# Sliding-window attention and a squared-ReLU feed-forward on one core: engine order from a list schedule, two batches turned on TensorE, two tiles in 128-token units, loads two batches ahead

## The chip, the cores and the metric

The kernel runs on one core of a Trainium2 chip. The core has TensorE (PE: matmuls, with its weight loads shown apart as PEld), VectorE (DVE), ScalarE (ACT), GpSimd (POOL) and SyncE (SP). Each engine takes its instructions strictly in program order, and semaphores order the engines against each other. Here POOL issues the loads from device memory, which turn float32 into bfloat16 on the way, and SP issues the copies inside the core's memory and the stores. The metric is device time in microseconds (us), lower is better. The kernel before takes 404.95 us, the median of 3 runs (404.74 to 405.19).

## The reference

Eight batches of 576 tokens with 8 heads of 64 go through attention in which a token sees the 32 tokens on either side of it. Its output, 4608 tokens by 512, goes through a feed-forward layer of width 2048.

```python
def _attn_ref(q, k, v):
    B, H, S, D = q.shape            # 8, 8, 576, 64
    scores = np.matmul(q, k.transpose(0, 1, 3, 2)) / np.sqrt(D)
    mask = np.abs(pos[:, None] - pos[None, :]) <= 32
    ...
    return np.matmul(attn, v)       # attn: softmax over the masked scores

def _moe_ref(x, w_in, w_out):       # x: 4608 x 512, w_in: 512 x 2048, w_out: 2048 x 512
    h = x @ w_in
    r = np.maximum(h, 0.0)
    return (r * r) @ w_out
```

## The kernel before

**Attention** goes in 72 steps, nine per batch, each for 64 query tokens and all heads. For a step, `scores(n)` makes four PE matmuls into one of two PSUM banks (`sc`), ACT takes the exponential, DVE multiplies by a mask into `pt`. `av(n)` makes eight matmuls with the values into the single bank `avp`; the last column of the values is one, so that the sums of the softmax come with it. DVE then takes reciprocals (`rs`) and scales (`xr`). `xturn(n)` turns the result by two PE transposes into `trp`, and ACT copies it to `xt`, which holds the tokens along the free axis.

**Queries and keys** must lie with the head's dimension on the partitions. A batch is loaded as rows by eight DMAs of POOL (`load_qk`, tiles `qraw`, `kraw`, two buffers), turned in 32x32 blocks by eight DVE stream transposes (`turn`, into `qst` and `kst`), and spread to its place by twelve DMAs of SP (`spread`, into `qz` and `kt`). The first `sc` matmul of a batch needs all twelve. Values need no turn: four DMAs to `vd` and two to `vx`, and SP copies the rest of `vx` out of `vd` (`copy_v`), since even steps need the rows shifted by 64.

**Feed-forward** goes in nine tiles of 512 tokens. `mm1(T, d)` makes four matmuls of 512 columns for one of 16 blocks of the width, ACT applies the ReLU (`rt`), DVE squares it (`gt`). `mm2(T, u, seg)` makes a quarter of the 16 matmuls that give 128 output tokens; after the last quarter ACT copies the bank (`oe`) and SP stores it. A unit of either is four matmuls.

**The order** is the order in which `build` records the operations; `rec` derives the waits from the tiles that are read and written, and `emit` writes the instructions out. In step n, `build` records `scores(n)`, one stream transpose of the next batch, a feed-forward unit, `xturn(n-2)`, a unit, `av(n-1)`, and two units. A unit of tile T may be recorded only once all eight steps of its tokens are through (`moe_items`), and `mm2` of a tile stands beside `mm1` of the next. At the start come the fills, the loads of batch 0, the fills of masks and identity, both weight matrices, and then the whole of batch 0's turns and spreads. Batch b+1 is loaded, as recorded, at steps 0 and 1 of batch b.

Of the kernel before, what the change touches and what calls it, by code (L numbers as in the profile page):

```python
# [3 lines left out]
ALU = mybir.AluOpType  # L4
# [12 lines left out]
VS = D_ + 2  # L17
KW = 32 + S_ + 32
LAST_MM = 16


class Op:
    __slots__ = ("eng", "fn", "deps", "same", "inc", "val", "sem", "dma")


class Prog:
# [3 lines left out]

    def __init__(self, nc):
        self.nc = nc
        self.ops = []
        self.writer = {}
        self.readers = {}
        self.dsem = {}

    def rec(self, eng, fn, reads=(), writes=(), dma=None):
        op = Op()
        op.eng, op.fn, op.dma = eng, fn, dma  # L40
        op.deps, op.same = set(), set()
        op.inc, op.val, op.sem = False, None, None
        for r in reads:
            for w in self.writer.get(r, ()):
                op.deps.add(w)
        for t in writes:
            for w in self.writer.get(t, ()):
                if not (w.eng == eng and w.dma is None and dma is None):
                    op.deps.add(w)
            for r in self.readers.get(t, ()):  # L50
                if not (r.eng == eng and r.dma is None):
                    op.deps.add(r)
        op.deps.discard(op)
        for r in reads:
            self.readers.setdefault(r, []).append(op)
        for t in writes:
            self.writer[t] = [op]
            self.readers[t] = []
        self.ops.append(op)
        return op  # L60

    def also_writes(self, op, *tiles):

        for t in tiles:
            self.writer.setdefault(t, []).append(op)
# [41 lines left out]
class Gen:  # L107
# [34 lines left out]
    def setup_v(self):  # L142
        p = self.p
        for i in range(2):
            for s, r in ((0, 0), (4, 64)):
                t = [("vx", i, s)]
                lo, hi = self.VX[i][r:r + 64, s, :, 0:64], self.VX[i][r:r + 64, s, :, 64:VS]
                p.rec("DVE", lambda e, a=lo: e.memset(a, 0.0), writes=t)
                p.rec("DVE", lambda e, a=hi: e.memset(a, 1.0), writes=t)

    def setup(self):
        p = self.p

        def ms(eng, t, ap, v):
            p.rec(eng, lambda e: e.memset(ap, v), writes=t)

        for i in range(2):
            for s in range(2):
                for hm in range(2):
                    o = 1 - hm  # L160
                    for dh in range(2):
                        r = 64 * dh + 32 * hm
                        ms("DVE", [("qz0", i, s, r)], self.QZ[i][r:r + 32, 2 * s:2 * s + 2, o, :], 0.0)
# [296 lines left out]
```

## Time and profile before

| what | value |
|---|---|
| median of 3 runs | 404.95 us |
| the profiled execution's own time | 405.0 us |
| its span, first to last instruction | 403.3 us |
| PE busy | 312.2 us, 77% |
| DVE busy | 217.9 us, 54% |
| ACT busy | 169.2 us, 42% |
| POOL busy | 84.9 us, 21% |
| read from and written to device memory | 36.70 MB and 9.44 MB |

The span is what the profile covers; the profiled execution took 1.7 us more than it. A busy share is an average over stages that have different limits, so the tables of single stretches say more than this table does. The duration of a matmul in a row runs from its start to the end of its pipeline, so the rate is read from the distance between starts, not from durations.

### The profile page before, as it was taken

The page shows a single profiled execution, that of the slowest core. Times are in us where ns is not written, and L with a number is a line of the kernel's source. Part 1 is how long each engine was busy: PE and PEld are TensorE (multiplying, and loading weights), DVE is VectorE, ACT ScalarE, POOL GpSimd, SP SyncE. Part 2 cuts the span into 40 slices and gives each one's busy share as a digit, 9 for nine tenths or more (in the row PEclk, how much of TensorE's full clock was granted, in tenths as well). Part 3 has the DMA queues.
Part 4 walks back from the last instruction along what each step waited for, and adds up shares of the span by engine and source line. Part 5 has one row for each costly group of instructions (what it writes and reads, how often), then busy time and mean ns, then how long its engine had stood idle before and what let it go on. Part 6 is the DMA issues. An engine that isn't in the chain of part 4 may idle for free.

```text
span 403.3 us, 5804 instructions
## 1 busy us (share of the span) xinstructions
PE 312.2 (77%) x2160; PEld 163.6 (41%) x2160; DVE 217.9 (54%) x460; ACT 169.2 (42%) x325; POOL 84.9 (21%) x140
## 2 busy tenths in 40 slices
PE   0002052895499969996999799988998999999996
PEld 0001041453245525553455345544554455544443
DVE  6940394499267735765477546764676344432200
ACT  1001041484145535563455345553655455544421
POOL 8994021511061005100511051101000000000000
PEclk9999999997599998999899989998999899999999
DMA  9999999786398456965695649374033000010112
GB/s 112 131 230 231 192 202 177 109 117 84 44 150 132 75 99 105 169 93 112 92 159 99 105 61 213 69 106 92 28 112 82 30 28 28 26 54 26 52 54 78
DMA packets 77531, 41.93 MB, mean 104 GB/s; under 512 B 41152, under 2 KB 71872, under 8 KB 77504
## 3 DMA queue, kind: packets, MB, share of 16 engines
q0 software_dynamic: 61312, 18.36, 43.8%
q1 hardware_dynamic: 16192, 23.21, 20.1%
q8 instruction: 17, 0.28, 0.3%
q14 instruction: 10, 0.08, 0.1%
HBM read 36.70 MB, written 9.44 MB: 114 GB/s over the span
## 4 chain that ended last, share of the span: by engine, by line
PE 69%; DMA 14%; DVE 8%; POOL 5%; ACT 1%; issue 1%; SPq 0%; ACTq 0%; DVEq 0%; POOLq 0%
PE ht L333 31%; PE outp L348 29%; DMA kt<-kst 7%; DMA qraw<-in_q_dram 6%; DVE kst L235 4%; PE sc L265 4%; PE trp L316 2%; PE avp L295 2%; PE avp L294 2%; DVE pt L280 1%; DVE xr L306 1%; DVE qst L235 1%; ACT e L273 1%; POOL qraw L194 1%; POOL vd L201 1%
## 5 line engine op out<-in xcount | busy, mean ns | idle before, releaser
L333 PE MATMUL ht<-xt,w 128*128 128x512 bf16 x576 | 154.6, 394 | 0.0
L348 PE MATMUL outp<-w,gt 128*128 128x512 bf16 x576 | 148.6, 386 | 0.0
L338 ACT ACTIVATE rt<-ht 128x512 bf16<-128x512 f32 x144 | 86.0, 597 | 107.0 <-PE ht L333 102.3
L340 DVE TENSOR_TENSOR gt<-rt 128x512 bf16<-128x512 bf16 x144 | 61.8, 430 | 60.4 <-ACT rt L338 59.3
L265 PE MATMUL sc<-qz,kt 128*128 128x128 bf16 x288 | 31.4, 240 | 63.2 <-DMA kt<-kst 63.2
L273 ACT ACTIVATE e<-sc 128x512 bf16<-128x512 f32 x72 | 42.8, 595 | 84.1 <-PE sc L265 73.6
L348 PEld LDWEIGHTS outp<-w,gt 128*128 128x128 bf16 x576 | 55.1, 100 | 56.5 <-issue 3.1
L280 DVE TENSOR_TENSOR pt<-e,mask 128x512 bf16<-128x512 bf16 x72 | 30.6, 424 | 83.6 <-ACT e L273 83.2
L333 PEld LDWEIGHTS ht<-xt,w 128*128 128x128 bf16 x576 | 51.2, 100 | 42.5 <-issue 5.0
L201 POOL DMA_DIRECT2D vd<-in_v_dram x32 | 28.2, 895 | 141.3 <-PE avp L295 112.5
L265 PEld LDWEIGHTS sc<-qz,kt 128*128 128x128 bf16 x288 | 23.2, 107 | 78.1 <-issue 54.6
L235 DVE STREAM_TRANSPOSE qst<-qraw 128x640 bf16<-128x640 bf16 (+1 forms) x32 | 46.3, 1464 | 11.8 <-DMA qraw<-in_q_dram 11.8
L235 DVE STREAM_TRANSPOSE kst<-kraw 128x640 bf16<-128x640 bf16 (+1 forms) x32 | 46.2, 1462 | 0.0
L316 PE MATMUL trp<-ident,xr 128*128 128x128 bf16 x144 | 22.1, 240 | 22.9 <-DVE xr L306 22.1
L320 ACT ACTIVATE xt<-trp 128x256 bf16<-128x256 bf16 x72 | 27.3, 379 | 20.0 <-PE trp L316 20.0
L306 DVE TENSOR_TENSOR xr<-avp,rs 128x256 bf16<-128x256 f32 x72 | 30.6, 424 | 2.7
L316 PEld LDWEIGHTS trp<-ident,xr 128*128 128x128 bf16 x144 | 14.2, 105 | 41.7 <-DVE xr L306 20.0
L356 ACT ACTIVATE oe<-outp 128x512 f32<-128x512 f32 x36 | 21.5, 597 | 19.9 <-PE outp L348 19.9
L194 POOL DMA_DIRECT2D qraw<-in_q_dram x32 | 19.6, 640 | 0.8 <-POOLq L445 0.8
L194 POOL DMA_DIRECT2D kraw<-in_k_dram x32 | 19.4, 641 | 0.0
L294 PE MATMUL avp<-vx,pt 128*128 128x65 bf16 x160 | 16.8, 204 | 2.0 <-DVE pt L280 2.0
L294 PEld LDWEIGHTS avp<-vx,pt 128*128 128x128 bf16 x160 | 14.2, 106 | 6.7 <-DVE pt L280 2.2
(26 smaller groups left out, 121.5 us busy)
## 6 DMA issues: line engine op xcount, KB each, us to landing
out_dram<-oe SPq DMA_DIRECT2D x36, 256.0 KB, 2.0
qraw<-in_q_dram POOLq DMA_DIRECT2D x32, 144.0 KB, 5.5
kraw<-in_k_dram POOLq DMA_DIRECT2D x32, 144.0 KB, 7.2
qz<-qst SPq DMA_DIRECT2D x64, 72.0 KB, 2.9
kt<-kst SPq DMA_DIRECT2D x32, 144.0 KB, 3.7
vx<-vd SPq DMA_DIRECT2D x16, 264.0 KB, 4.9
vd<-in_v_dram POOLq DMA_DIRECT2D x32, 128.0 KB, 4.9
w<-in_moe_w_in_dram POOLq DMA_DIRECT2D x4, 512.0 KB, 9.9
```

The costliest lines, as they stand in the source:

```text
L194: self.p.rec("POOL", lambda e, g=g, s=s: e.dma_start(raw[32 * g:32 * g + 32], s), writes=[("raw", t, b % 2, g)], dma=(f"{t}{b % 2}", b))
L235: self.p.rec("DVE", lambda e: e.transpose(dst, src), reads=[("raw", t, i, g) for g in range(4)], writes=[("st", t, dh, m0)])
L265: mm = e.matmul(sc[:, 128 * j:128 * j + 128], self.KT[i][:, j, 64 * c:64 * c + 128], self.QZ[i][:, j, :, 64 * c:64 * c + 64], start=True, ...
L273: self.p.rec("ACT", lambda e: e.activation(self.E[n % 2][:], sc[:], ACTF.Exp, scale=0.125), reads=[("sc", n % 2)], writes=[("e", n % 2)])
L280: self.p.rec("DVE", lambda e: e.tensor_tensor(pt, ee, mb, ALU.mult), reads=[("e", n % 2), ("mask", mi)], writes=[("pt", n % 2)])
L294: e.matmul(o, pt[:, 192 * j:192 * j + 128], vt[:, ha, 0:VE], start=True, stop=False)
L306: self.p.rec("DVE", lambda e: e.tensor_tensor(bass.AP(xr, 0, [[256, 128], [64, 4], [1, 64]]), bass.AP(self.AVP, 0, [[512, 128], [VE, 4], [ ...
L316: mm = e.transpose(self.TRP[:, 128 * t:128 * t + 128], xr[:, 128 * t:128 * t + 128], self.ID[:])
L333: mm = e.matmul(ht[:], self.W1[:, ft, 128 * d:128 * d + 128], self.XT[:, ft, 512 * T:512 * T + 512], start=(ft == 0), stop=(ft == 3))
L338: self.p.rec("ACT", lambda e: e.activation(rt[:], ht[:], ACTF.Relu), reads=[("ht", k % 2)], writes=[("rt", k % 4)])
L340: self.p.rec("DVE", lambda e: e.tensor_tensor(gt[:, d, :], rt[:], rt[:], ALU.mult), reads=[("rt", k % 4)], writes=[("gt", T % 2, d)])
L348: mm = e.matmul(op[:], gt[:, d, 128 * u:128 * u + 128], self.W2[:, d, :], start=(d == 0), stop=(d == 15))
```

## The change

The operations and their waits stay as a model, but the order no longer comes from the recording. `rec` now takes for each operation a duration, a priority (`key`, low first) and for DMAs a transfer time. `schedule` goes through all operations engine by engine: whenever an engine is free, it takes of the operations whose inputs are there the one with the lowest key. `emit` then writes them in the order of these planned starts, so each engine still runs a fixed list. Attention of step n has the key n - 10, unit d of tile T the key 8T + d/2.

Batches 0 and 1 are loaded in three pieces of 192 tokens each, in rows of four tokens (`fine_load`, 48 partitions). `fine_turn` turns a piece by 16 PE transposes of 48 columns into an `sc` bank; four copies, on ACT for queries and on DVE for keys, take it to `qz` or `kt`. Stream transposes and spreads remain for batches 2 to 7. The first pieces lie in tiles not yet in use (`gt`, `qraw`, `kraw`, `xt`). The scores of a step wait only for the pieces that they read, and each `av` only for its own rows of the values. Tiles 0 and 1 go through `mm1_small`: 16 matmuls of 128 columns for 128 tokens and four blocks of the width, in the same bank and with the same ACT and DVE work per unit. From batch 2 on, queries and keys of batch b have the key 9b - 40, their transposes a key near 9b - 16.

On POOL, the loads at the start stood so before (the first is for queries, then keys, values in `vd` and `vx`, rows of one batch):

```order
L194 DMA qraw<-in_q_dram 32x9x256 x4
L194 DMA kraw<-in_k_dram 32x9x256 x4
L201 DMA vd<-in_v_dram 128x8x64 x4
L204 DMA vx<-in_v_dram 32x8x64
L207 DMA vx<-in_v_dram 32x8x64
```

They stand so now, on the same engine at the same place:

```order
L262 DMA gt<-in_k_dram 48x8x256
L262 DMA gt<-in_q_dram 48x8x256
L313 DMA vd<-in_v_dram 128x8x64
L352 DMA w<-in_moe_w_in_dram 128x4x512
L207 ISA
L207 AFFINE_SELECT ident<-ident 128x128
L325 DMA vx<-in_v_dram 96x8x64
L207 AFFINE_SELECT ident<-ident 128x128
L207 AFFINE_SELECT mask<-mask 128x64 x5
L262 DMA qraw<-in_k_dram 48x8x256
L262 DMA gt<-in_q_dram 48x8x256
L352 DMA w<-in_moe_w_in_dram 128x4x512
```

A third of batch 0's keys and queries, a quarter of the values and a quarter of the first weights now stand ahead of the rest.

On PE, the first feed-forward unit stood so before, after the scores of the eleventh step (`ht` is the bank of `mm1`):

```order
L265 MATMUL sc<-qz,kt 128x128 x4
L333 MATMUL ht<-xt,w 128x512 x4
L316 MATMUL trp<-ident,xr 128x128 x2
L333 MATMUL ht<-xt,w 128x512 x4
L294 MATMUL avp<-vx,pt 128x65
```

It stands so now, behind the second step's `av` (L276 are the transposes of a piece, L488 the small units):

```order
L276 MATMUL sc<-ident,qraw 128x48 x16
L467 MATMUL trp<-ident,xr 128x128 x2
L276 MATMUL sc<-ident,gt 128x48 x16
L488 MATMUL ht<-xt,w 128x128 x16
L411 MATMUL sc<-qz,kt 128x128 x12
L488 MATMUL ht<-xt,w 128x128 x16
```

Feed-forward units moved ahead of all but two steps of attention; they need the results of two steps, not eight.

On DVE, a stretch of batch 2's attention had a square of the feed-forward (`gt`) on either side of each transpose before (the numbers tell buffers apart):

```order
L280 TENSOR_TENSOR pt0<-e0,mask0 128x4x2x64
L235 STREAM_TRANSPOSE kst<-kraw1 128x4x4x32
L340 TENSOR_TENSOR gt1<-rt0 128x512
L304 RECIPROCAL rs1<-avp 128x4
L306 TENSOR_TENSOR xr1<-avp,rs1 128x256
L340 TENSOR_TENSOR gt1<-rt1 128x512
L280 TENSOR_TENSOR pt1<-e1,mask0 128x4x2x64
```

In the change, batch 2's steps stand with batch 3's transposes and no squares between:

```order
L423 TENSOR_TENSOR pt0<-e0,mask0 128x4x2x64
L366 STREAM_TRANSPOSE qst<-qraw1 128x4x4x32
L454 RECIPROCAL rs1<-avp 128x4
L423 TENSOR_TENSOR pt1<-e1,mask0 128x4x2x64
L456 TENSOR_TENSOR xr1<-avp,rs1 128x256
L366 STREAM_TRANSPOSE kst<-kraw1 128x5x4x32
L454 RECIPROCAL rs0<-avp 128x4
```

The squares moved out of this stretch, since tile 1's are through before it and tile 2's need its steps.

The core of the diff:

```diff
+LEAD = 10
+NSMALL = 2
+TOFF, TST, TREL = 6, 0.9, 11
+NQ = 48
+PC = 4 * NQ
...
+    def schedule(self):
...
+            t, e = best
+            while wait[e] and wait[e][0][0] <= t:
+                _, i, op = heapq.heappop(wait[e])
+                heapq.heappush(pool[e], (op.key, i, op))
+            op = heapq.heappop(pool[e])[2]
+            op.start = t
+            free[e] = t + op.dur
+            op.end = t + op.dur + op.lat
...
+        self.ops = sorted(out, key=lambda o: (o.start, o.i))
...
+    def fine_load(self, b, t, x, key):
+        h, row, base = self.fine_raw(b, t, x)
+        src = (self.q if t == "q" else self.k)[b]
+        s = src[:, PC * x:PC * x + PC, :].rearrange("h (p t) d -> p h (t d)", t=4)
+        d = bass.AP(h, base, [[row, NQ], [256, 8], [1, 256]])
+        self.p.rec("POOL", lambda e: e.dma_start(d, s), writes=[("fraw", b, t, x)], dma=(f"f{b}{t}{x}", 0), key=key,
+                   dur=700, move=1440)
...
+    def fine_turn(self, b, t, x, key):
...
+                        mm = e.transpose(ps[:, to:to + NQ], bass.AP(h, at, [[row, NQ], [1, 128]]), self.ID[0:NQ, 0:NQ])
...
+                if t == "q":
+                    self.p.rec("ACT", lambda e, d=dst, c=src: e.activation(d, c, ACTF.Copy),
+                               reads=[tag] + ([w] if par else []), writes=[w], key=key, dur=480)
+                else:
+                    self.p.rec("DVE", lambda e, d=dst, c=src: e.tensor_copy(d, c),
+                               reads=[tag] + ([w] if par else []), writes=[w], key=key, dur=480)
...
+    def mm1_small(self, T, g, q, key):
...
+            for d in range(4 * q, 4 * q + 4):
+                for ft in range(4):
+                    mm = e.matmul(ht[:, 128 * (d % 4):128 * (d % 4) + 128], self.W1[:, ft, 128 * d:128 * d + 128],
+                                  self.XT[:, ft, t0:t0 + 128], start=(ft == 0), stop=(ft == 3))
...
+        self.p.rec("PE", f, reads=[("xt", 8 * T + 2 * g), ("xt", 8 * T + 2 * g + 1), ("w1", q)], writes=[("ht", k % 2)], key=key,
+                   dur=900)
...
-            moe(1)
-            if n >= 2:
-                self.xturn(n - 2)
-            moe(1)
-            if 1 <= n <= NSTEP:
-                self.av(n - 1)
-            moe(2)
-            done = n - 2
-        moe(len(items))
...
+        self.fine_load(0, "k", 0, K)
+        self.fine_load(0, "q", 0, K + 1)
...
+            if b > 1:
+                kb = 9 * b - 40
+                self.load_qk(b, "q", kb)
+                self.load_qk(b, "k", kb)
...
+                self.scores(n)
+                self.av(n)
+                self.xturn(n)
...
+        for T in range(1, NT + 1):
+            for d in range(16):
+                key = 8 * T + d / 2
+                if T < NSMALL:
+                    self.mm1_small(T, d // 4, d % 4, key)
+                elif T < NT:
+                    self.mm1(T, d, key)
+                self.mm2(T - 1, d // 4, d % 4, key + 0.25)
+        p.schedule()
```

458 lines of the change are left out of this document (302 added, 156 removed).

## The prediction

> **What bounds the kernel now.** I began with the busy times of three long stretches (columns: length; then PE, PEld, DVE, ACT and POOL busy with instruction counts; granted clock; DMA share; GB/s).
>
> ```profile
> span 403.3 us, 5804 instructions
> ...
> 0.00:108.00 108.00, 35.95 (x311) 23.08 (x312) 63.47 (x129) 27.01 (x52) 45.94 (x82) 0.94 1.13 152
> 108.00:315.00 207.00, 190.97 (x1352) 99.17 (x1351) 128.86 (x266) 103.86 (x202) 38.94 (x58) 0.95 0.62 105
> 315.00:400.27 85.27, 85.23 (x499) 41.33 (x497) 25.62 (x66) 37.75 (x70) 0.00 (x0) 0.99 0.11 41
> ```
>
> PE is busy without a gap in the last stretch, nearly so in the middle, and a third of the time in the first. So the kernel is three kernels: a start that waits, a middle that PE bounds with holes, an end that PE bounds alone. What a PE unit costs I read from starts in the timeline of PE, around the border of two batches:
>
> ```profile
> 139.75 1.02 PE L333 MATMUL ht<-xt,w 128*128 128x512 bf16 x4
> ...
> 141.48 0.39 PE L265 MATMUL sc<-qz,kt 128*128 128x128 bf16 x4
> 141.70 1.03 PE L333 MATMUL ht<-xt,w 128*128 128x512 bf16 x4
> 142.56 0.28 PE L316 MATMUL trp<-ident,xr 128*128 128x128 bf16 x2
> 142.68 1.03 PE L348 MATMUL outp<-w,gt 128*128 128x512 bf16 x4
> 143.54 0.19 PE L294 MATMUL avp<-vd,pt 128*128 128x65 bf16 x1
> ...
> 143.79 1.02 PE L333 MATMUL ht<-xt,w 128*128 128x512 bf16 x4
> 144.65 1.03 PE L348 MATMUL outp<-w,gt 128*128 128x512 bf16 x4
> 149.54 0.38 PE L265 MATMUL sc<-qz,kt 128*128 128x128 bf16 x4 [3.87 <-DMA kt<-kst]
> 149.76 1.82 PE L333 MATMUL ht<-xt,w 128*128 128x512 bf16 x4
> 151.37 0.42 PE L316 MATMUL trp<-ident,xr 128*128 128x128 bf16 x2
> 151.59 1.86 PE L348 MATMUL outp<-w,gt 128*128 128x512 bf16 x4
> 153.28 0.19 PE L294 MATMUL avp<-vx,pt 128*128 128x65 bf16 x1
> ```
>
> Four scores take 0.22 us (55 ns each), four matmuls of 512 columns 0.86 (216 ns), two transposes 0.11, eight `av` matmuls 0.24 (30 ns each, a load of 128 weight columns before every one). With 1152 matmuls of 512 columns and 72 attention steps, PE has 1152 x 0.216 + 72 x (0.22 + 0.24 + 0.11) = 248.8 + 41.0 = **289.8 us** of work at full rate. The same rows show the hole: PE is through at about 145.5, waits until 149.54 for the spread keys, and then needs 3.74 us to 153.28 for units that take 2.05, since the first two units run at half rate. A border thus costs 4.0 + 1.7 = 5.7 us. The waits and the chain that ended last name the cause and the end:
>
> ```profile
> PE sc L265 <- DMA kt<-kst: 63.2, 8, 33.3
> ...
> 143.22 1.23 DVE kst L235
> 145.11 4.29 DMA kt<-kst
> ...
> 385.56 14.69 PE outp L348 x68
> ...
> 400.33 0.60 ACT oe L356
> ```
>
> Eight such waits hold 63.2 us, the longest 33.3 at the start. A batch's last transpose starts late on DVE, because one stands in each step, and its copies then take 4.29 us with PE idle. After PE's last matmul (400.25) 3.05 us remain for the last copy and store.
>
> The ledger of before: 403.3 - 289.8 - 3.05 = 110.5 us lost. Between 108 and 315, 16.0 us are idle (207 - 190.97), and five half-rate starts of 1.7 make 8.5, so 24.5 are lost there. None is after 315. The start has lost the remaining **86 us**.
>
> **The change, part by part.** *PE work added.* Twelve turns of 16 transposes at 30 ns (weight load of 128 columns and 48 moving, nearest the `av` row) are 12 x 0.48 = 5.8 us. The 32 small units have 16 matmuls of 128 columns at 55 ns = 0.88 us against 0.86, together 0.5. PE work becomes 289.8 + 6.3 = **296.1**. Bounds: a turn's matmul between 30 ns and the 55 of a 128-column one, up to 4.8 us more.
>
> The Trainium skill, "TensorE: Matmul & The Clock Gate", Back-to-back issue gap, speaks against the small units: it gives about 81 ns per matmul of 128 columns as the sustained spacing in a stream of weight loads and matmuls, and 131 ns at 512 columns. The trace has 55 and 216, so the row decides; by the page the 512 small matmuls would cost 512 x 26 ns = 13 us more, an estimate.
>
> *The start.* What can PE do before data is there? Loads go in order, at the rates of two stretches before, batch 0's loads and the weights:
>
> ```profile
> 2.25:14.25 12.00, 0.00 (x0) 0.00 (x0) 9.18 (x25) 0.00 (x0) 11.44 (x29) 1.00 1.56 147
> 16.50:30.00 13.50, 0.00 (x0) 0.00 (x0) 8.30 (x7) 0.00 (x0) 13.50 (x21) 1.00 1.17 215
> ...
> GB/s 112 131 230 231 192 202 177 109 117 84 44 150 132 75 99 105 169 93 112 92 159 99 105 61 213 69 106 92 28 112 82 30 28 28 26 54 26 52 54 78
> ...
> 1.35 2.52 POOL L194 DMA_DIRECT2D qraw<-in_q_dram  x4 [0.83 <-POOLq L445]
> ...
> 6.23 3.52 POOL L201 DMA_DIRECT2D vd<-in_v_dram  x4
> ...
> 14.43 3.01 POOL L222 DMA_DIRECT2D w<-in_moe_w_in_dram  x4
> ```
>
> In bytes written, batch 0 is 1.77 MB (12.0 us at 147 GB/s) and `w_in` 2.10 MB (9.8 at 215). POOL needs 0.63 to 0.88 us per issue, and keeps ahead of that. Batch 0 and `w_in` end at 2.25 + 21.8 = 24 us, the first two quarters of `w_out` at 29.4, all of `w_out` at 34, batch 1 at 46. I add 1.5 us for the landing (choice; a lag of 3 would move the start by 1.5). In the order, PE's second `mm2` unit stands ahead of the last two of batch 0's `av`-transpose pairs and needs the second quarter of `w_out`: 31 us. Until then PE has done 6 turns, 9 scores, 6 `av`, 5 transposes, 4 small units and one `mm2`: 2.9 + 2.0 + 1.4 + 0.6 + 3.5 + 0.9 = 11.3 us. **Lost 20 us** where 86 were. Batch 0's loads at 112 GB/s, the page's first slice, would add 3.8 us; at 215 they would take 3.8 off.
>
> After 31 us the units queue up. Half rate after the wait costs 1.7. The first turn of batch 1 is reached at about 39 us (8 us of PE work behind the 31) and its data lands at 37, so arrivals no longer bind. The copies behind a turn do, once:
>
> ```profile
> L273 ACT ACTIVATE e<-sc 128x512 bf16<-128x512 f32 x72 | 42.8, 595 | 84.1 <-PE sc L265 73.6 <-DVE gt L340 10.2 <-DVE pt L280 0.2
> L306 DVE TENSOR_TENSOR xr<-avp,rs 128x256 bf16<-128x256 f32 x72 | 30.6, 424 | 2.7
> ...
> L320 ACT ACTIVATE xt<-trp 128x256 bf16<-128x256 bf16 x72 | 27.3, 379 | 20.0 <-PE trp L316 20.0
> ```
>
> A copy of 384 elements lies between 379 ns (256) and 595 (512), I take 0.49, so four are 2.0 us; behind batch 1's last turn PE has 1.1 us of other work. With the `av` chains of both batches on one bank I take **4 us** for these (0 to 8).
>
> *Batch 2.* As the order shows, its steps stand on DVE with batch 3's transposes and nothing else to give PE. The same mix ran before, in batch 0 without feed-forward:
>
> ```profile
> 49.28 0.41 DVE L280 TENSOR_TENSOR pt<-e,mask 128x512 bf16<-128x512 bf16 x1
> ...
> 53.74 0.41 DVE L280 TENSOR_TENSOR pt<-e,mask 128x512 bf16<-128x512 bf16 x1
> ...
> L340 DVE TENSOR_TENSOR gt<-rt 128x512 bf16<-128x512 bf16 x144 | 61.8, 430 | 60.4 <-ACT rt L338 59.3
> L235 DVE STREAM_TRANSPOSE kst<-kraw 128x640 bf16<-128x640 bf16 x16 | 25.7, 1603 | 0.0
> L235 DVE STREAM_TRANSPOSE kst<-kraw 128x512 bf16<-128x512 bf16 x16 | 21.1, 1320 | 0.0
> ...
> qraw<-in_q_dram POOLq DMA_DIRECT2D x32, 144.0 KB, 5.5
> ```
>
> Two steps with two transposes take 4.46 us, so the six steps that tile 2 needs take 13.4. An exponential and a mask ahead of them and a turn and copy behind, 0.6 + 0.4 and 0.1 + 0.4 with their hand-overs some 2 us, make 15.4. PE has there eight `mm2` units, nine scores, six `av` and six transposes, 6.9 + 2.0 + 1.5 + 0.7 = 11.1. **4 us** lost (2 to 8).
>
> *Later borders.* The 24.5 us of holes go where the last transpose of a batch comes 5.1 us (from 144.45, its end, to 149.54) ahead of the first scores. Counted in units of the new order, it stands 8.4 us of PE work ahead for batch 4, of which ReLU (0.6, like the exponential), square (0.43) and transpose (1.32) take 2.4, so 6.0 us stand against 5.1, about even; for batch 3 it is tight too, from batch 5 on there are 11 us and more. I take **3 us** (0 to 8). In all else the steady step of before lost nothing: its 4.04 us (139.75 to 143.79) equal 4 x 0.864 + 0.57.
>
> DVE gets 24 copies of keys of 0.5 us and loses 16 of its 64 transposes; ACT gets the 24 copies of queries. Neither is late next in the middle: DVE had 25.8 us of work per batch there (128.86 over five), against 36.2 of PE (289.8 over eight). The fills that moved from POOL to DVE lie beside the first loads.
>
> The sum: 296.1 + 20 + 1.7 + 4 + 4 + 3 + 3.05 = 331.9 us of span; the profiled execution took 1.7 us beside its span (405.0 against 403.3), and 405.0 is 0.05 above the median shown. **333.5 us.**
>
> **Rivals.** *Small units at a dearer rate.* If in a long stream a weight load no longer hides behind a matmul of 128 columns, its 30 ns (the `av` spacing) come on top of the 55: 512 x 30 ns are 15 us, and the time is 349. Against it: four scores in 0.22 us, each with its own load. Chance 0.08. By the 81 ns of the Trainium skill's page above it would be 347.
>
> *Tight waits.* The list is greedy: attention with its low keys is put where the plan has its inputs just ready, so whatever is later on the chip stalls PE. If each of the 48 stream transposes, 1.3 to 1.6 us long, holds up an `av` for half a microsecond, that is 24 us; with 3 already counted, 354. For it: DVE at 71% (25.8 of 36.2), one `avp` bank. Against it: before, the same transposes stood in every step and cost nothing. The holes at the borders staying (24.5) would give 355, the case in which the new order doesn't do what it says. Chance 0.17 for 346 to 375.
>
> *Faster.* All loads at 215 GB/s, no stalls in batches 0 to 4: 333.5 - 3.8 - 11 = 319. Chance 0.04 below 320.
>
> *Slower than before.* POOL's queue is in order, and loads of values, which wait for PE's `av` two batches earlier, now stand between loads of keys. If a load of keys is held so that it starts only when its predecessor's attention is over, the chain of load (5.5 us to landing), eight transposes (11.7) and spread (5.1) is open, 22.3 us at each of six borders: 134 us, and 464 in all. It passes the time of before only if over 12 us of each chain, 72 in all, are open. Against it: keys are loaded at 9b - 40, far ahead. Chance 0.02.
>
> **How the numbers follow.** Forecast 0.69 (320 to 346), dear small units 0.08, tight waits 0.17, faster 0.04, slower 0.02. The range 319 to 352 takes in the forecast, the small units and the near end of the tight waits, some 0.82. Faster by over 0.2%, which is about what a measurement of this kernel can tell from no change, 0.97; within it 0.01; slower 0.02.
>
> **What would show it.** PE's first turn near 6 us, its second `mm2` unit waiting for `w_out` near 31; PE busy some 95% from 40 us on, with a hole of some 4 us in batch 2 while DVE is full; no wait of 4 us for `kt` at a border; starts in a small unit 55 ns apart at full rate. It would be wrong if PE is starved past 40 us, if small matmuls stand 80 ns apart, or if `av` waits for DVE in every step.

## The result, and the profile after

The changed kernel takes **346.3 us** (median of four runs, 344.7 to 348.3); the kernel before took 405.1 beside it (404.7 to 405.7). The ratio is 0.855, with a 95% interval of 0.850 to 0.860. The forecast was 333.5 with a range of 319 to 352: the direction and the bulk of the gain came, 58.8 us in place of 71.5, and 12.8 us are missing. The profiled execution took 346.9 us, with a span of 345.2. One execution of `again` and one of `extra` (both below) ran in a slower state, and the medians and ranges given for these two leave it out.

The page of the changed kernel: the busy time of each engine, then PE's busy share and its granted clock in 40 slices of 8.6 us, in tenths.

```profile
span 345.2 us, 6957 instructions
...
PE 312.3 (90%) x2736; PEld 183.1 (53%) x2736; DVE 204.8 (59%) x468; ACT 180.9 (52%) x349; POOL 82.8 (24%) x130
...
PE   1457699999989679998999999999999999999996
...
PEclk9995689999999899999999999999999999999999
```

PE now works from the first slice, is nearly full from the sixth on, and has one dent left, above all the slices 14 and 15 (112 to 129 us). The stretches (length; PE, PEld, DVE, ACT, POOL; clock; DMA share; GB/s) show the same in numbers:

```profile
0.00:31.00 31.00, 13.64 (x188) 11.01 (x188) 18.66 (x59) 13.17 (x23) 29.75 (x53) 0.89 1.32 164
31.00:60.00 29.00, 25.52 (x382) 21.88 (x383) 14.79 (x36) 15.94 (x32) 10.23 (x16) 0.82 2.08 175
60.00:90.00 30.00, 29.44 (x403) 21.92 (x400) 24.98 (x52) 19.25 (x39) 7.11 (x10) 1.00 1.02 137
90.00:120.00 30.00, 24.65 (x234) 14.80 (x232) 24.29 (x43) 13.26 (x26) 10.46 (x16) 0.94 1.04 188
...
180.00:240.00 60.00, 60.00 (x443) 31.79 (x441) 40.61 (x87) 34.17 (x68) 5.87 (x8) 1.00 0.56 109
240.00:290.00 50.00, 50.00 (x381) 26.77 (x379) 24.48 (x66) 27.73 (x56) 0.00 (x0) 1.00 0.11 39
```

From 180 to 290 us nothing is idle: the borders of the late batches are closed. From 90 to 120 PE misses 5.35 us while DVE works 24.29 of 30; this stretch holds the border to batch 2 and most of batch 2's steps. PE's waits (total, times, longest):

```profile
PE trp L467 <- DVE xr L456: 9.4, 8, 3.0
...
PE sc L411 <- DVE kt L295: 3.9, 1, 3.9
PE sc L411 <- DMA kt<-kst: 3.7, 2, 2.1
```

The 63.2 us for spread keys have become 3.7. What leads now is the wait of a step's turn for the normalised result `xr` of DVE, 9.4 us in eight places.

To place what is lost I use one ledger for all kernels. "Lost" at an event is its start less the PE work that stands ahead of it in PE's order, at the full-rate prices (216 ns for 512 columns, 55 to 56 for 128, 30 for an `av` matmul, 31 for a turn's). Events: the fifth step's copy to `xt`, and the first exponentials of batches 1, 2 and 3. Each figure is worked out from the profiled execution of that kernel; where a trace lacks the record of a matmul, its whole unit is counted all the same:

| kernel | xt, step 5, at | lost there | batch 1 | batch 2 | batch 3 | end |
|---|---|---|---|---|---|---|
| changed | 39.5 us | 29.2 | 32.8 | 35.9 | 44.2 | 45.6 |
| changed, run again | 38.5 | 28.3 | 30.7 | 32.3 | 41.7 | 43.1 |
| fills | 39.6 | 29.3 | 30.7 | 33.6 | 42.5 | 44.1 |
| warm | 39.2 | 29.0 | 31.1 | 32.6 | 41.5 | 45.2 |
| extra | 41.7 | 31.4 | 33.8 | 35.3 | 43.7 | 45.4 |
| vfirst | 37.8 | 27.6 | 32.1 | 32.9 | 45.1 | 47.9 |
| direct | 31.0 | 22.1 | 30.8 | 43.1 | 55.9 | 57.3 |
| b3later | 39.0 | 28.7 | 31.1 | 32.9 | 41.5 | 42.8 |
| b3xr | 39.1 | 28.8 | 32.4 | 35.3 | 44.1 | 46.5 |
| late | 38.6 | 28.4 | 31.3 | 33.3 | 44.5 | 68.4 |

For the changed kernel 296.6 us of work, 45.6 lost and the tail of 3.0 make its 345.2. The forecast had 32.7 lost: 20 + 1.7 + 4 until batch 1 is through, 4 in batch 2, 3 at later borders. So about 10 of the missing 13 us lie ahead of batch 2. The start of the changed kernel, as PE's timeline has it (a row every few us; the wait of 2.57 us put down to "issue" ends when a copy of values lands, at 25.6):

```profile
5.88 1.59 PE L276 MATMUL sc<-ident,gt 48*128 48x48 bf16 x32 [5.88 <-POOL ident L207]
...
17.61 1.89 PE L488 MATMUL ht<-xt,w 128*128 128x128 bf16 x16
...
25.65 0.21 PE L438 MATMUL avp<-vx,pt 128*128 128x65 bf16 x1 [2.57 <-issue]
...
30.20 0.40 PE L467 MATMUL trp<-ident,xr 128*128 128x128 bf16 x2 [1.45 <-DVE xr L456]
31.28 1.04 PE L411 MATMUL sc<-qz,kt 128*128 128x128 bf16 x8 [0.69 <-ACT qz L292]
...
39.05 0.40 PE L467 MATMUL trp<-ident,xr 128*128 128x128 bf16 x2 [3.02 <-DVE xr L456]
39.69 3.60 PE L529 MATMUL outp<-w,gt 128*128 128x512 bf16 x8
```

The first turn stands at 5.88, as forecast. But the first two `mm2` units stand at 39.69, not at 31, and wait for no `w_out`: what they wait behind, in PE's order, is the chain of batch 0's attention. The DMA issues of the weights show that the loads were late too (per issue in ns min/median/max, first and last start; then landing after issue, min/median/max), `w_out` of the changed kernel:

```profile
L357 POOL DMA_DIRECT2D w<-in_moe_w_out_dram x4: 797/801/816, 14.8 to 17.5; - x4
...
DMA to landing us min/median/max: 17.0/20.4/24.3
```

All of `w_out` is there at 17.5 + 24.3 = 41.8 us, where the forecast had 34. From the landing of the first quarter (14.8 + 17.0 = 31.8) on, the other three took 10 us, 3.3 each of 0.52 MB: 157 GB/s, not 215.

### The profile page after: what moved, and what is told of

Same layout as the page of the kernel before. It is cut to its first block, busy times and chain, and to the rows that moved or that the text cites. A ratio compares the mean times of both kernels' runs of the same rounds, so it can differ in the third digit from the quotient of the medians.

```text
span 345.2 us, 6957 instructions
## 1 busy us (share of the span) xinstructions
PE 312.3 (90%) x2736; PEld 183.1 (53%) x2736; DVE 204.8 (59%) x468; ACT 180.9 (52%) x349; POOL 82.8 (24%) x130
## 4 chain that ended last, share of the span: by engine, by line
PE 78%; DVE 10%; DMA 6%; ACT 3%; issue 2%; SPq 0%; ACTq 0%
PE outp L529 32%; PE ht L511 26%; PE ht L488 7%; PE sc L411 5%; DMA kt<-kst 4%; DVE kst L366 3%; PE avp L438 3%; PE trp L467 3%; PE avp L439 3%; DMA vx<-vd 2%; DVE qz L204 2%; ACT qz L292 1%; DVE kt L295 1%; PE sc L276 1%; DVE xr L456 1%
## 5 line engine op out<-in xcount | busy, mean ns | idle before, releaser
L529 PE MATMUL outp<-w,gt 128*128 128x512 bf16 x576 | 144.8, 382 | 0.0
L511 PE MATMUL ht<-xt,w 128*128 128x512 bf16 x448 | 115.2, 383 | 0.2 <-ACT xt L471 0.2
L519 DVE TENSOR_TENSOR gt<-rt 128x512 bf16<-128x512 bf16 x112 | 46.6, 418 | 43.8 <-ACT rt L517 43.3
L511 PEld LDWEIGHTS ht<-xt,w 128*128 128x128 bf16 x448 | 40.8, 99 | 39.1 <-issue 2.1
L313 POOL DMA_DIRECT2D vd<-in_v_dram x32 | 28.8, 909 | 87.2 <-PE avp L439 60.6
L411 PE MATMUL sc<-qz,kt 128*128 128x128 bf16 x288 | 28.3, 229 | 8.6 <-DVE kt L295 3.9
L488 PE MATMUL ht<-xt,w 128*128 128x128 bf16 x512 | 34.8, 227 | 0.9 <-ACT rt L494 0.7
L366 DVE STREAM_TRANSPOSE kst<-kraw 128x640 bf16<-128x640 bf16 (+1 forms) x24 | 35.0, 1459 | 0.0
L366 DVE STREAM_TRANSPOSE qst<-qraw 128x640 bf16<-128x640 bf16 (+1 forms) x24 | 34.7, 1461 | 0.0
L536 ACT ACTIVATE oe<-outp 128x512 f32<-128x512 f32 x36 | 21.6, 599 | 23.9 <-PE outp L529 23.9
L488 PEld LDWEIGHTS ht<-xt,w 128*128 128x128 bf16 x512 | 31.4, 102 | 2.9 <-ACT rt L494 0.9
L411 PEld LDWEIGHTS sc<-qz,kt 128*128 128x128 bf16 x288 | 21.0, 103 | 18.4 <-DVE kt L295 4.0
L454 DVE RECIPROCAL rs<-avp 128x4 f32<-128x4 f32 x72 | 13.4, 186 | 23.6 <-PE avp L439 22.9
L494 ACT ACTIVATE rt<-ht 128x512 bf16<-128x512 f32 x32 | 19.0, 598 | 13.2 <-PE ht L488 11.4
```

The source lines that it names most:

```text
L313: self.p.rec("POOL", lambda e, s=s: e.dma_start(self.VD[i][:, s, :, 0:64], v[b, :, 32 + 128 * s:160 + 128 * s, :].rearrange("h p d -> p h ...
L366: self.p.rec("DVE", lambda e: e.transpose(dst, src), reads=[("raw", t, i, g) for g in range(4)], writes=[("st", t, dh, m0)], key=key, dur= ...
L411: mm = e.matmul(sc[:, 128 * j:128 * j + 128], self.KT[i][:, j, 64 * c:64 * c + 128], self.QZ[i][:, j, :, 64 * c:64 * c + 64], start=True, ...
L488: mm = e.matmul(ht[:, 128 * (d % 4):128 * (d % 4) + 128], self.W1[:, ft, 128 * d:128 * d + 128], self.XT[:, ft, t0:t0 + 128], start=(ft == ...
L511: mm = e.matmul(ht[:], self.W1[:, ft, 128 * d:128 * d + 128], self.XT[:, ft, 512 * T:512 * T + 512], start=(ft == 0), stop=(ft == 3))
L519: self.p.rec("DVE", lambda e: e.tensor_tensor(gt[:, d, :], rt[:], rt[:], ALU.mult), reads=[("rt", k % 4)], writes=[("gt", T % 2, d, u) for ...
```

## The experiments

Each was timed against the kernel before on its own chip; all ratios are to that kernel.

**fills: is it DVE's order?** In the changed kernel two fills of a query tile wait on DVE for the scores of batch 0's last step, ahead of the work that the fifth step needs (timeline of DVE):

```profile
35.13 1.02 DVE L204 MEMSET qz<- 32x1152 uint32 x1 [2.08 <-PE sc L411]
36.44 1.02 DVE L204 MEMSET qz<- 32x1152 uint32 x1 [0.29 <-issue]
...
38.57 0.42 DVE L456 TENSOR_TENSOR xr<-avp,rs 128x256 bf16<-128x256 f32 x1
```

PE's wait of 3.02 us at 39.05 is for that `xr`. The two fills and batch 1's first fills were given an earliest place:

```diff
-        self.setup_qz(1, -30, [(0, 64, 0), (64, 64, 1)])
+                if n == 1:
+                    self.setup_qz(1, -30, [(0, 64, 0), (64, 64, 1)], (), [self.masked[1]])
...
-                              [(t, b - 2, x, hm) for t in ("qf", "kf") for x in range(3) for hm in range(2)])
+                              [(t, b - 2, x, hm) for t in ("qf", "kf") for x in range(3) for hm in range(2)],
+                              [self.masked[9 if b == 2 else 15]])
```

> Two fills of qz on DVE are held back by a dependency: batch 1's behind the second mask of batch 0, batch 2's behind the first mask of batch 1. Order theory (fills stand on DVE ahead of work that PE waits for): about 1.4 us at the first copies of keys and 2.3 us at the fifth step go, the time lost by PE before 43 us falls from 31 to about 27, and the kernel from 346.3 to about 342.5 us. Arrival theory (PE follows the landings anyway): the same place is reached at the same time, 345.5 to 347.

343.9 us (342.0 to 345.5), ratio 0.848 (0.843 to 0.853). The fills are gone from their place, yet the fifth step comes at the same time:

```profile
39.28 0.29 PE L467 MATMUL trp<-ident,xr 128*128 128x128 bf16 x2 [1.65 <-DVE xr L456]
```

So the fills are not what the start waits for by themselves; the interval overlaps the changed kernel's, and a gain of up to 2 us is neither shown nor excluded. The median lies between the two expectations.

**warm: is it the clock?** PE's granted clock is low while it waits in the start. Eighty groups of four matmuls, whose result nothing reads, keep it busy; they have the lowest rank, so they are put only where PE would idle.

```diff
+        for i in range(80):
+            self.idle(i)
...
+            for _ in range(4):
+                mm = e.matmul(op[:, 0:128], self.ID[:], self.ID[:], start=True, stop=True)
...
+        self.p.rec("PE", f, reads=["id"], writes=[("outp", 1)], key=1000.0 + i, dur=224)
```

> 80 groups of four extra matmuls of identity by identity into an unused bank, which nothing reads, stand in PE's idle places of the first 40 us. If the half rate of PE holds the start up: the first small units take 0.9 us and not 1.8, about 7 us of PE work on the chain halves, and the kernel gains 2 to 4 us (342 to 344). If landings and the copies behind them set the start: 346 within 1 us, with the fifth step's copy at 39 us as before; the extra groups themselves cost at most 0.4 us where they stand ahead of work.

347.7 us (346.0 to 351.1), ratio 0.859 (0.853 to 0.865). The first 43 us, first of the changed kernel, then of this one:

```profile
0.00:43.00 43.00, 22.34 (x262) 17.38 (x263) 23.45 (x70) 17.53 (x31) 33.74 (x58) 0.82 1.47 170
```

```profile
0.00:43.00 43.00, 35.74 (x618) 33.38 (x619) 24.47 (x73) 18.01 (x33) 33.97 (x58) 1.00 1.43 172
```

The clock rises from 0.82 to 1.00 and a small unit takes 1.06 us in place of 1.89, but the fifth step stands at 39.2 us as before. Up to there half rate costs nothing that shows: PE's own work is not on the path. Behind the fifth step it does count. The first two `mm2` units, 3.60 us in the changed kernel's row at 39.69, take 1.89 here:

```profile
39.27 1.89 PE L539 MATMUL outp<-w,gt 128*128 128x512 bf16 x8
```

That is 1.7 us less, but the time shows no gain, and its median lies somewhat above the 346 within 1 that was expected if landings set the start.

**extra: is it the arrivals?** One more weight quarter stands ahead of batch 0's second pieces.

```diff
         self.load_v(0, K + 3, 0)
+        self.load_extra(K + 4.5)
```

`load_extra` loads the last quarter of `w_out`, as `load_w2(3, ...)` does again later.

> One more load of 512x512 float32 elements (the fourth quarter of w_out, loaded a first time in this place and again at its own) stands in the load queue ahead of the second pieces of batch 0's keys and queries; nothing else changes and no result depends on it. Theory (the start follows the arrival of batch 0's loads, and a weight quarter moves in about 3.6 us): everything of batch 0 behind it lands about 3.6 us later, the fifth step's tokens reach xt at about 43 us instead of 39.5, and the time is 348.5 to 351. Rival (the start is held by what the engines do between the landings, so that a later landing is partly absorbed): 346 to 347.5.

347.2 us (346.0 to 348.7), ratio 0.856 (0.852 to 0.859), beside 0.850 (0.846 to 0.854) for the changed kernel on the same chip (`again`, below). The median lies in the rival's range, 346 to 347.5, and the intervals touch. The fifth step's copy on ACT, first in the changed kernel run again, then here:

```profile
38.54 0.38 ACT L471 ACTIVATE xt<-trp 128x256 bf16<-128x256 bf16 x1 [0.19 <-PE trp L467]
```

```profile
41.68 0.38 ACT L476 ACTIVATE xt<-trp 128x256 bf16<-128x256 bf16 x1 [0.19 <-PE trp L472]
```

It is 3.1 us later than in that profile and 2.2 later than in the first one (39.5); the second pieces of keys and queries landed at 17.1 and 17.8, where those two have 14.5 to 14.7 and 15.0 to 16.0. So the fifth step follows a landing that is put off, by 2 to 3 us of the 3.6, where two executions of one order differ by 1.0 (next). The time does not show it: by batch 2 35.3 us are lost, between the 32.3 and 35.9 of the changed kernel's two profiles. This supports the theory for the fifth step and leaves its worth open.

**again: how far do two executions of one order lie apart?** No edit.

> The changed kernel with no edit at all, beside the other two on the same chip. If its order alone sets its time, 345 to 348 with about 33 us lost by the first exponential of batch 1; a profile that loses 1 to 2 us more or less there shows how far two executions of one order lie apart.

345.1 us (342.7 to 346.3), ratio 0.850 (0.846 to 0.854). The same order lost 32.3 us by batch 2 in this profile and 35.9 in the first. `w_out` came earlier, issued at the same times:

```profile
L357 POOL DMA_DIRECT2D w<-in_moe_w_out_dram x4: 810/818/829, 14.8 to 17.5; - x4
...
DMA to landing us min/median/max: 15.5/18.9/21.8
```

The last quarter landed at 39.3 in place of 41.8. The loads' rate differs from one execution to the next, and some of the spread of 3.7 us among the changed kernel's runs may come from it; differences of up to some 3.6 us between single profiles in the table are not to be read.

**vfirst: the attention's loads ahead of the weights.**

```diff
+        self.load_v(0, K + 6, 1)
-        self.load_w1(1, K + 6)
-        self.load_v(0, K + 7, 1)
-        self.load_w1(2, K + 8)
+        self.load_w1(1, K + 7)
+        self.load_w1(2, K + 13)
...
-        self.load_w1(3, K + 10)
+        self.load_w1(3, K + 14)
```

> All of batch 0's values, keys and queries are loaded ahead of the third and fourth quarter of w_in, and its second block of values ahead of the second quarter too; the bytes are the same. Theory (the values and the second and third pieces of keys and queries, with the copies of values that can only follow them, set when the first eight steps of attention run): the second block of values lands about 3.6 us earlier, and the last loads of batch 0's attention 5 to 7 us earlier, the fifth step's copy to xt stands near 34 to 36 us instead of 39.5, and the time falls by 2 to 5 us, to 341.5 to 345. Rival (the sum of the bytes bounds the start, whatever their order, because the small units then wait for w_in's later quarters): 346 to 348, with as much lost by the first exponential of batch 1 (about 33 us) as in the changed kernel.

348.8 us (346.9 to 350.4), ratio 0.859 (0.855 to 0.863). No gain; `again`, on the same chip, has 0.846 to 0.854, so this order is about 1% slower. The loss ahead of batch 1 (32.1) lies between those of the two profiles of the changed kernel. The second block of values landed at 17.1 in place of 18.7 us. But the copy from it, on SP's queue beside the loads, was issued 1.6 us earlier and landed only 0.9 earlier; first the changed kernel (issue at 19.2, landed 6.3 later), then this one:

```profile
L346 SPq DMA_DIRECT2D vx<-vd x1: 597/597/597, 19.2 to 19.2; - x1
...
DMA to landing us min/median/max: 6.3/6.3/6.3
```

```profile
L346 SPq DMA_DIRECT2D vx<-vd x1: 597/597/597, 17.6 to 17.6; - x1
...
DMA to landing us min/median/max: 7.0/7.0/7.0
```

And where the third pieces were early (24.0 and 25.1 us became 21.0 and 21.9), the same two fills on DVE held the fifth step, now with PE's wait of 2.02 us for `xr` behind them:

```profile
34.24 1.02 DVE L204 MEMSET qz<- 32x1152 uint32 x1 [2.13 <-PE sc L411]
35.55 1.02 DVE L204 MEMSET qz<- 32x1152 uint32 x1 [0.29 <-issue]
```

The theory that the order of the loads alone would bring 2 to 5 us is wrong, though part of its premise failed too: the second block of values landed 1.6 us earlier, not 3.6, and the third pieces about 3, while only the last values came 5 us and more earlier.

**direct: all of them at once.** The edits of `fills`, `vfirst` and `b3later` (below), two blocks of values by loads of their own in place of copies, and 3500 in place of 2700 ns for a weight quarter in the plan.

```diff
+        self.load_vx(K + 5.5, 1)
...
+        self.load_vx(K + 8.5, 2)
...
-        for s in range(4):
+        for s in (2, 3):
             self.copy_v(0, -50 + s, s, s + 1)
...
-                   writes=[("w1", d)], dma=(f"w1{d}", 0), key=key, dur=770, move=2700)
+                   writes=[("w1", d)], dma=(f"w1{d}", 0), key=key, dur=770, move=3500)
```

> Every cause that the runs before pointed to is taken away at once: the fills of the query tiles stand where DVE is free (as in fills), the attention's loads of batch 0 stand ahead of the third and fourth quarter of w_in (as in vfirst), two blocks of values come by loads of their own in place of copies from one tile to another that landed 6 to 7 us after their issue, batch 3's turns start later (as in b3later), and the scheduler is told 3.5 us for a weight quarter in place of 2.7. Theory (each of landing, copy and fill holds batch 0's chain in turn, so that taking away one alone only uncovers the next): the fifth step's copy to xt comes at 30 to 33 us instead of 38.5 to 39.5, 24 to 29 us are lost by the first exponential of batch 1 instead of 31 to 33, and the time is 335 to 341. Rival (the bytes set the start: with the chain earlier, the small units wait for the later quarters of w_in and the first second-matmul units for w_out, which then land 2 us later): the fifth step earlier as well, but 30 us or more lost by the first exponential of batch 1, and 342 to 346.

356.5 us (353.4 to 358.6), ratio 0.879 (0.876 to 0.883): worse than either expected. The first half of the theory came true, the fifth step's copy is 7.5 to 8.5 us earlier:

```profile
30.99 0.38 ACT L479 ACTIVATE xt<-trp 128x256 bf16<-128x256 bf16 x1
31.49 2.44 ACT L292 ACTIVATE qz<-sc 64x384 bf16<-64x384 bf16 x4
34.50 1.09 ACT L424 ACTIVATE e<-sc 128x512 bf16<-128x512 f32 x2 [0.56 <-PE sc L419]
```

But the lead is gone by batch 1 (30.8 lost, as the rival had it, though not by the rival's cause: from 30 to 66 us PE waits 4.8 us, for copies, `xr`, `xt` and an exponential, and for no weights). The plan put three small units and the steps of the first tokens ahead of the turns of the third pieces, and the next scores wait for the four copies above. What cost the time lies later: 12.3 us between batches 1 and 2, 12.8 between 2 and 3. In the chain of waits batch 1's `xr` now stand with the transposes of batch 2, and the key copies come late and slow:

```profile
83.77 0.42 DVE xr L464
84.20 1.52 DVE qst L374
85.72 0.26 DVE pt L431
85.97 0.33 DVE xr L464
86.30 1.22 DVE qst L374
...
102.89 7.59 DMA kt<-kst
```

These two stretches lose 25.1 us where the changed kernel loses 11.4. An edit of the start moves the order of all that follows, and here the middle cost more than the start could bring. Which of the edits did it is not shown: `b3later`'s, which is meant for batch 3 and took 344.2 us by itself, and the longer plan time for weights are among them.

**late: what loading two batches ahead is worth.** In the plan, keys and queries of a batch may be loaded only once the steps of the batch before it have begun. This moves their place in POOL's order; no wait on the chip goes with it.

```diff
-                self.load_qk(b, "q", kb)
-                self.load_qk(b, "k", kb)
+                self.load_qk(b, "q", kb, [self.masked[9 * b - 9]])
+                self.load_qk(b, "k", kb, [self.masked[9 * b - 9]])
```

(`load_qk` passes the list on as the record's `after`, and the low load of values has a semaphore name of its own.)

> Queries and keys of batches 2 to 7 are loaded no earlier than the first mask of the batch before (as the kernel before the change did), all else stays. If loading two batches ahead is what closes the borders, holes of up to 4 us and a half-rate start of 1.7 come back at up to six borders: 355 to 375 us. Rival: the order of the transposes alone closes them (load 5.5, transposes 11.7, spread 5.1 make 22 us, less than the 36 us of a batch): 345 to 349 us, and the spreads land faster.

370.1 us (369.6 to 373.1), ratio 0.914 (0.910 to 0.920): 24 us slower than the changed kernel. The holes at the borders are back:

```profile
PE sc L411 <- DMA kt<-kst: 19.4, 5, 5.9
```

Between batch 3 and the end 23.9 us are lost in place of 1.4. The borders are closed by the loads two batches ahead, and not by the list order alone. How is less clear than the expectation has it. Batch 4's loads were issued from 123.3 us on, where the changed kernel has 85.7; that is still some 11 us ahead of batch 3's first mask (134.0). Its rows had all landed by 136.5. Yet its transposes ran only from 142.7 to 160.4 (127.4 to 150.7 in the changed kernel). Batch 5's loads, issued from 159.3 on, then ran beside its last key copies, of which the last took 8.2 us. Later transposes and slower copies came together here, and no run separates them.

**b3later and b3xr: batch 2's hole.** In the changed kernel batch 3's transposes stand on DVE among batch 2's steps. In `b3later` they are allowed only from batch 2's seventh step on; in `b3xr` only behind its sixth step's `xr`.

```diff
-[self.masked[min(9 * b - TREL + st, 9 * b - 1) if b > 2 else 12 + st // 2]])
+[self.masked[(24 + st // 4 if b == 3 else min(9 * b - TREL + st, 9 * b - 1)) if b > 2 else 12 + st // 2]])
```

```diff
+[self.xrs[23] if b == 3 else self.masked[min(9 * b - TREL + st, 9 * b - 1) if b > 2 else 12 + st // 2]])
```

> Batch 3's eight transposes are held behind batch 2's steps 24 and 25. If DVE with those transposes is what PE waits for in batch 2, the 8 us lost between 100 and 124 us fall to 2 or 3 and the kernel takes 340 to 343 us. Rival: the transposes are then late for batch 3, whose first scores wait for kt by 5 us or more: 346 or above, with the loss moved to the border.

> Batch 3's transposes are held behind the scaling (xr) of step 23, so that none stands among the steps that tile 2 needs. If transposes on DVE are what PE waits for in batch 2: the loss from the first exponential of batch 2 to the 24th copy to xt falls from 4.1 us (change) and 6.3 (run b3later) to 1 or less, and if batch 3 is in time nonetheless, the kernel takes 340 to 342 us. Rival: the steps are a chain on one avp bank, and the 4 us stay; or the loss moves to batch 3's first scores, 344 to 346.

`b3later` took 344.2 us (343.8 to 345.6), ratio 0.850 (0.846 to 0.854), not the 340 to 343 expected; `b3xr` 346.8 (344.4 to 348.1), ratio 0.855 (0.851 to 0.859). In both, 8.6 to 8.8 us are lost between the first scores of batches 2 and 3, against 8.3 and 9.4 in the changed kernel. In `b3later` the transposes still fall in one stretch ahead of two steps' `xr` (PE waits 11.8 us for `xr` in all); PE then waits for no keys at batch 3. In `b3xr` 2.2 us are lost up to the sixth step, against 4.1, and 6.6 from there to batch 3, against 4.2. Only 1.3 of these 6.6 are a wait for keys at batch 3; PE waits as well for the `xr` of the next two steps (2.2) and for a ReLU (0.7). The hole is DVE's work at a place where PE has little else. Moving the transposes moves it, as `b3xr`'s rival said, but to batch 2's last steps more than to batch 3's first scores.

**small9 and big0: the small units.** All nine tiles in 128-token units, and none.

```diff
-NSMALL = 2
+NSMALL = 9
```

> All nine tiles in units of 128 tokens: 7 x 256 more matmuls of 128 columns in place of 7 x 64 of 512. If a matmul with its weight load takes 55 ns: 7 x (256 x 0.0555 - 64 x 0.216) = 2.7 us more, 349. If the weight load does not hide (85 ns): 7 x 7.9 = 55 us more, about 400; at 81 ns some 48 us more, 395.

> No tile in 128-token units: tile 0's first matmuls wait for eight steps, whose last copy to xt comes at about 48 us, while the change has 9 us of small units done by then. If the small units are what fills the start: 352 to 356 us. Rival: PE has other work to bring forward (second matmuls, batch 1) and the end of the start is set by landings: 346 to 349.

`small9` took 350.1 us (348.3 to 350.9), ratio 0.863 (0.859 to 0.867). Consecutive rows of PE give the price:

```profile
150.49 1.06 PE L488 MATMUL ht<-xt,w 128*128 128x128 bf16 x16
151.38 1.03 PE L529 MATMUL outp<-w,gt 128*128 128x512 bf16 x4
152.24 0.28 PE L467 MATMUL trp<-ident,xr 128*128 128x128 bf16 x2
```

Sixteen in 0.89 us are 55.6 ns each, and 0.86 for four of 512 columns: seven more tiles cost 2.7 us of PE work (299.3 against 296.6 by the ledger's prices), and the time is 350. The dear rate of the forecast's rival would have given 400. The Trainium skill, "TensorE: Matmul & The Clock Gate", Back-to-back issue gap, has 81 ns for this shape in a stream; by it the 1792 small matmuls added would have cost 1792 x 25 ns = 45 us more than at 55.6 ns, an estimate. The time rose by 3.8 in all; the measurement decides against it here.

`big0` (`NSMALL = 0`, tile 0 in units of 512 tokens as well) took 348.7 us (347.0 to 348.8), ratio 0.859 (0.856 to 0.862). It loses 37.6 us by batch 1, five to seven more than the changed kernel's two profiles, and 48.2 at the end, 2.6 to 5.1 more: part of what PE could not do early cost nothing later. The time is what the rival expected. By the medians the small units bring about 2 us, which is within what the runs differ.

**fb1: batch 1 on DVE and SP, as batches 2 to 7 are.** Only batch 0 is turned on TensorE.

```diff
-        if b < 2:
+        if b < 1:
...
+            if b == 1:
+                for st in range(8):
+                    self.turn(b, t, dh, 5 * m, 5 + 4 * m, 9 * b - LEAD - TOFF + st * TST, [self.masked[2 + st // 2]])
```

> Batch 1 goes by stream transposes on DVE and spreads, as batches 2 to 7; batch 0 stays on TensorE. Its rows land at about 50 us, eight transposes take 11.7 us and the spreads 5 to 8, so its first scores come at about 68 us in place of 57. PE has then 16 second matmul units of tile 0 (13.8 us) to fill with: the kernel takes 346 to 349 us. If that work is not there in time (the list has it, but the weights land at 42 us and tile 0 is done at 57): 353 or above.

355.7 us (354.6 to 357.7), ratio 0.878 (0.875 to 0.882). Batch 1's first scores move from 57 to 75.6 us, 40.1 are lost by then, 57.9 at the end, with 3.0 us less of PE work. It is the case that the expectation put at 353 or above. Turning batch 1 on PE, with its loads in pieces, is worth 9.4 us net.

No edit beat the changed kernel by more than the runs differ; `fills` and `b3later`, 2 us below it, are within that.

## Why the prediction was right, and where it was off

- *PE work, 296.1.* Right: 296.6 in the ledger. A small matmul is spaced 55.6 ns and a turn's transposes 31 ns at full rate.
- *The start, 20 us lost, bound by the second quarter of `w_out` at 31.* This is the term that failed. At the fifth step's copy, just ahead of the first `mm2` units, the two profiles have lost 29.2 and 28.3 us. The losses at the end exceed the forecast by 12.9 and 10.4, so this term is most of what is missing. Two steps were wrong. First, the rate of the weights: 215 GB/s was what all queues moved in that stretch. The trace of before has the landings that I didn't look at:

```profile
L222 POOL DMA_DIRECT2D w<-in_moe_w_in_dram x4: 760/765/776, 14.4 to 16.7; - x4
...
DMA to landing us min/median/max: 5.5/9.9/14.9
```

The first quarter landed at 19.9 and the last at 31.6, 3.9 us for each 0.52 MB, or 134 GB/s, while SP's spreads ran beside them. In the changed kernel the second quarter of `w_out` landed at 35.4 us, and at 33.9 in the second profile, not at 31. (By its own rates the forecast should have had the first two quarters at 28.9, not 29.4.) Second, what binds: PE reached its second `mm2` unit only at about 41 us, 40 in the second profile, and waited for no weights there. The chain was batch 0's own: second pieces at 14.7 and 16.0, the values' copies at 25.6 (they took 6 us beside the loads, and the forecast had them at nothing), four copies of 0.60 us behind each turn in place of 0.49, and DVE's fills waiting in the queue. `direct` took several of these away and the fifth step came 7.5 to 8.5 us earlier; `fills`, `vfirst` and `warm`, one each, moved it by 2 at most. What of the start each is worth is not settled, nor whether an order exists that keeps `direct`'s lead.
- *Half rate, 1.7 us, and copies, 4 us.* Right in size: from the fifth step to batch 2 6.7 and 4.0 us are lost, where the two terms make 5.7. The half rate cost 1.7 in the first profile's two `mm2` units and none in `warm`, whose time was no better. Of the rest 1.6 us in the first profile are a wait for the spread keys of batch 2, which the forecast did not have.
- *Batch 2, 4 us, with DVE full of batch 3's transposes.* Right: up to the sixth step of batch 2, which tile 2 needs, 4.1 us are lost (the ledger goes from 35.9 to 40.0), 4.0 in the other profile, and the waits are for `xr`. The first row below is the longest of three such waits, the second is the border to batch 3:

```profile
114.25 0.28 PE L467 MATMUL trp<-ident,xr 128*128 128x128 bf16 x2 [1.57 <-DVE xr L456]
...
123.57 0.40 PE L411 MATMUL sc<-qz,kt 128*128 128x128 bf16 x4 [2.10 <-DMA kt<-kst]
```

- *Later borders, 3 us.* From batch 2's sixth step to batch 3 4.2 and 5.4 us are lost, of which 2.1 and 3.3 are the wait for keys: the forecast had called this border tight, with 5.1 us for the spread, and the key copies took 7.35 (last section). Most of the rest is half rate behind batch 2's waits, since 12 matmuls of 512 columns take 4.1 us from 116.81 on, and 2.6 at full rate. From batch 3 to the end only 1.4 more are lost. `late` shows that the loads ahead are needed for this, since without them the borders reopen for 24 us, near the 24.5 of before.
- *Rivals.* Dear small units are ruled out by `small9`. The tight waits exist (9.4 us in eight waits for `xr`), but only in the start and in batch 2: from 180 us on PE lost none. Slower than before has no sign: even with the loads held back, `late` stays 35 us below the kernel before.
- *The range.* 346.3 lies within 319 to 352, but just outside the 320 to 346 that the forecast kept for its own account. The room that took it in was there for dear small units, which did not come, and for the near end of the tight waits; that a slow start fell into it is partly luck.
- *Where the gain comes from.* The span is 58.1 us shorter. By the same ledger the kernel before has lost 83 us at the first exponential of batch 2 and 27.5 behind it (the prediction put 86 to the start), where the changed kernel has 35.9 and 9.7. So the start gives 47 us, what follows 17.8, and 6.8 of PE work were added. `fb1` is worth 9.4 of the start and `big0` about 2. No run goes back to the old order of the list or to stream transposes for batch 0, so how the rest of the start's gain divides between the list order, the loads in pieces and the turns on TensorE is not shown.

## What to carry to other kernels

A rate read from a stretch's total belongs to all queues in it; for one stream read the landings, and price a copy from one tile to another beside a backlog of loads by such a copy, not at nothing. A chain that is held in turn by an arrival, a copy and a queue in order may hardly get shorter when one of them is removed, as here, so list what is late next before crediting a removal. A greedy list order has to be timed as a whole: `direct`, whose edits were mostly meant for the start, lost 14 us more between batches 1 and 3.

## What the hardware showed that was not expected

Copies from tile to tile were slower than the row that the forecast priced them by. The key spreads, 144 KB each, that the prediction's rows had at 4.29 us from the transposes to the last landing took 7.14 and 7.35 in the changed kernel's chain, with loads of later batches in the queue:

```profile
93.80 7.14 DMA kt<-kst
...
116.18 7.35 DMA kt<-kst
```

PE waited for them at these two borders alone. The chain of the kernel before has a slow one as well, at batch 1, while loads of rows and values were still landing:

```profile
64.98 7.21 DMA kt<-kst
```

At its later borders it has 2.57 to 4.29. So slow copies stood beside loads in both kernels, but no experiment separated the loads from other causes. And one order of instructions loads at a different pace from one execution to the next: all of `w_out` was there at 41.8 us in one profile and at 39.3 in another, with equal issue times to a tenth of a microsecond.
